# Conv then low-rank mixer on one core: eight-tile conv with shifted copies on GpSimd, eight output buffers, batch 0 in two pieces

## The chip, the core and the metric

The kernel runs on one core of a Trainium2 chip. Its engines are TensorE (PE, with weight loads shown as PEld), VectorE (DVE), ScalarE (ACT), GpSimd (POOL) and SyncE (SP). The metric is the time of one execution on the device in microseconds, as the median of several runs. A profile is one further execution, taken by the hardware profiler; its rows give durations of single instructions and what ended an engine's idle time.

## The reference

`x` is 8 batches of 4224 positions of 192 channels. First comes a causal convolution along the positions: 8 heads of 24 channels, 7 taps for each head, softmaxed. Then a mixer: a rank-32 product along the positions, added to its input, and a two-layer net along the channels, added again.

```python
w = exp(weight - max) / (sum + 1e-9)              # 8 heads x 7 taps
y[b, s, h, :] = sum_k w[h, k] * x_pad[b, s + k, h, :]   # 6 zeros ahead
h = y.transpose(0, 2, 1) @ U @ V                  # U: 4224 x 32, V: 32 x 4224
u = y + h.transpose(0, 2, 1)
out = u + maximum(u @ w_ch1, 0) @ w_ch2           # 192 -> 768 -> 192
```

## The kernel before, in words

**Tiles.** A batch is 33 tiles of 128 positions; 264 tiles in all, in 33 groups of 8. Everything after the load is bf16, sums are fp32 in PSUM. PSUM is one ring of eight banks (`bank`, line 55), handed out in program order, so that an instruction that wants a bank waits for the one that emptied it eight banks before.

**Load.** `x_part` (line 75) loads part of a batch from fp32 to bf16 on GpSimd's DMA queue. In SBUF, partitions 0 to 63 hold the blocks of 64 positions of the first half of the batch (32 blocks and one for the halo), partitions 64 to 127 those of the second (34 and one). A batch is four parts (`XP`, line 83); batch 0 is loaded and convolved in three pieces instead (`KP`, line 85, and `x_piece`). Three x buffers rotate. The parts of batches 2 to 7 are issued from the main loop, held until a certain matmul of W1 is done (`LOADS`, line 607).

**Conv** (line 297) is matmuls with a band matrix as the weights: for each head, one product for the block itself and one for the halo, the block before it (`halo`), for each half `r` and for even and odd blocks `c`. These are 64-by-64 tiles of the array, four (`r`, `c`) side by side; each has up to 17 blocks of 24 channels, 408 columns. That makes 8 matmuls a head and 64 a batch. Each head fills two banks, and `evac` copies them to `y_sb`, one on ACT and one on DVE (engines "AD").

**U product and h.** `tt_mm` (line 334) multiplies y by U in 33 small matmuls on 128-by-32 tiles; `tt_split` and `tt_sum` bring it to the form that h needs. `h_group` (line 448 on) makes the 8 tiles of h for one group (L425), and DVE adds y (L447) to give u. A DMA transpose on SP's queue turns u round for W1 (`transp`).

**W1 and W2.** `w1` (line 511) makes 36 matmuls of 512 columns for a group, with ReLU on ACT and DVE by a pattern (L530, L532). `w2` (line 537) makes two tiles at a time in 12 matmuls of 192 columns; DVE adds u into an output buffer (L551), and SP stores it (L558). Four output buffers rotate (line 51).

**Order.** It is written out by hand. Each entry of `SLOTS` (line 571) lists the groups for W1, the groups for W2, the convs that come between the two, and what is done ahead of which W2 step: `h` makes an h group, `t` the U product, `s` its sum. Slots 5 to 13 have three groups each (24 tiles); the convs of slots 5 to 10 are in `CONV`. Each engine works through its instructions in program order.

**Start.** 60 matmuls on zeros (`idle`, line 170) run first; the band is built; then three and two idle matmuls of 512 columns stand ahead of the first and second piece of batch 0 (lines 620 and 623).

Of the kernel before, what the change touches and what calls it, by code (L numbers as in the profile page):

```python
# [14 lines left out]
def kernel(  # L15
# [10 lines left out]
    nc = tc.nc  # L26
# [16 lines left out]
    ctx.enter_context(tc.manual_schedule())  # L43

    cst = ctx.enter_context(tc.tile_pool(name="cst", bufs=1))
    xs = ctx.enter_context(tc.tile_pool(name="xs", bufs=3))
    ys = ctx.enter_context(tc.tile_pool(name="ys", bufs=3))
    us = ctx.enter_context(tc.tile_pool(name="us", bufs=7))
    uts = ctx.enter_context(tc.tile_pool(name="uts", bufs=5))
    rls = ctx.enter_context(tc.tile_pool(name="rls", bufs=3))  # L50
    outs = ctx.enter_context(tc.tile_pool(name="outs", bufs=4))
    sml = ctx.enter_context(tc.tile_pool(name="sml", bufs=2))
    psp = ctx.enter_context(tc.tile_pool(name="psp", bufs=8, space=bass.MemoryType.PSUM))

# [14 lines left out]
    def x_tile(b):  # L69
        xt[b] = xs.tile([P, NB1 + 1, D], BF16, name="x_sb")  # L70
# [11 lines left out]

    XP = [(0, 1, 17), (0, 17, NB0 + 1), (1, 0, 18), (1, 18, NB1 + 1)]

    KP = [(0, 7), (7, 13), (13, NB1 // 2)]

    def x_piece(k):
        for r in range(2):
            k0, k1 = KP[k]
            k1 = min(k1, (NB0, NB1)[r] // 2)  # L90
            x_part(0, r, (1 - r if k == 0 else 2 * k0 + 1), 2 * k1 + 1)
# [25 lines left out]

    fp = cst.tile([P, P], I32, name="fp")
    nc.gpsimd.iota(fp[:], pattern=[[1, P]], base=P, channel_multiplier=-1)
    x_piece(1)  # L120

    efp = cst.tile([P, 4, P], I32, name="efp")
    nc.gpsimd.iota(efp[:], pattern=[[-1, 4], [1, P]], base=4 * P, channel_multiplier=-4)
# [8 lines left out]
    )  # L132
    nlast = NT * 32 - nfull * P
    nc.gpsimd.dma_start(out=Ur[0:nlast, nfull, :], in_=U4[nfull * P :, :])
    x_piece(2)


    V0_sb = cst.tile([32, 2 * GT * P], BF16, name="V0_sb")
# [155 lines left out]
            )  # L294


    def conv(b, h0, nh, rs, engs, k0=0, k1=NT):

        if yt[b] is None:
            yt[b] = ys.tile([P, NT, D], BF16, name="y_sb")  # L300
        nk = {r: min(k1, (NB0, NB1)[r] // 2) - k0 for r in rs}
        pp = {r: bank() for r in rs}
        w = nh * GS
        for hh in range(nh):
            h = h0 + hh
            for halo in range(2):
                for r in rs:
                    for c in range(2):
                        st = 1 - halo + c + 2 * k0
                        nc.tensor.matmul(  # L310
                            out=pp[r][HB * c : HB * c + HB, 0 : nk[r] * w].rearrange(
                                "p (k a) -> p k a", a=w
                            )[:, :, hh * GS : hh * GS + GS],
                            lhsT=band[HB * r : HB * r + HB, h, HB * halo : HB * halo + HB],
                            rhs=xt[b][
                                HB * r : HB * r + HB,
                                st : st + 2 * nk[r] - 1 : 2,
                                h * GS : h * GS + GS,
                            ],
                            start=(halo == 0),  # L320
                            stop=(halo == 1),
                            tile_position=(HB * r, HB * c),
                        )
        for n, r in enumerate(rs):
            j0 = NB0 // 2 * r + k0
            evac(
                engs[n % len(engs)],
                yt[b][:, j0 : j0 + nk[r], h0 * GS : h0 * GS + w],
                pp[r][:, 0 : nk[r] * w].rearrange("p (k a) -> p k a", a=w),
            )  # L330
# [55 lines left out]
            )  # L386

    def tt_done(b, p):
        t = sml.tile([P, D], BF16, name="tt_sb")
        nc.vector.tensor_copy(out=t[:], in_=p[:, 0:D])  # L390
        ttb[b] = t

# [167 lines left out]
    def held(ins, after):  # L560
        tc.add_manual_dep(
            ins.ins,
            after.ins.name,
            mybir.DependencyInfo(mybir.DependencyClass.Sync, mybir.DependencyReason.DATA),
            reason="load held back",
        )
# [2 lines left out]


    SLOTS = [
        ([0], [], [], {}),
        ([1], [0], [], {0: ["h0"], 1: ["h3"]}),
        ([2], [1], [(1, 0, 8)], {0: ["h1"], 1: ["t1"], 3: ["s1"], 4: ["h4"]}),
        ([3], [2], [(2, 0, 4)], {1: ["h5"]}),
        (
            [4, 5],
            [3, 4, 5],
            [(2, 4, 8)],
            {1: ["t2", "h6"], 3: ["s2"], 4: ["h7"], 7: ["h8"], 10: ["h9"]},  # L580
        ),
    ]
    CONV = {
        5: [(3, 0, 8)],
        6: [(4, 0, 8)],
        7: [(5, 0, 4)],
        8: [(5, 4, 8), (6, 0, 3)],
        9: [(6, 3, 8), (7, 0, 2)],
        10: [(7, 2, 8)],
    }  # L590
    SUMS = {5: (3, 5), 6: (4, 10), 8: (5, 2), 9: (6, 6), 10: (7, 10)}
    nh = 10
    for k in range(5, 14):
        gs = list(range(3 * k - 9, 3 * k - 6))
        at = {}
        for p in (1, 5, 9) if k == 5 else (2, 6, 10):
            if nh < NG:
                at.setdefault(p, []).append(f"h{nh}")
                nh += 1
        if k in SUMS:  # L600
            b, p = SUMS[k]
            at.setdefault(p, []).insert(0, f"t{b}")
            at.setdefault(p + 2, []).insert(0, f"s{b}")
        SLOTS.append((gs, gs, CONV.get(k, []), at))
    assert nh == NG

    LOADS = {2: [(1, 5), (1, 5), (2, 2), (2, 5)]}
    for b, g in ((3, 4), (4, 6), (5, 9), (6, 12), (7, 15)):
        LOADS[b] = [(g, 1), (g, 4), (g + 1, 1), (g + 1, 4)]

    def held(ins, after):
        tc.add_manual_dep(
            ins.ins,
            after.ins.name,
            mybir.DependencyInfo(mybir.DependencyClass.Sync, mybir.DependencyReason.DATA),
            reason="load held back",
        )


    idle(3, 512)  # L620
    for h in range(0, H, 2):
        conv(0, h, 2, [0, 1], "AD", *KP[0])
    idle(2, 512)
    for h in range(0, H, 2):
        conv(0, h, 2, [0, 1], "AD", *KP[1])
    u_layout()
    yT = yT_part(0)
    jb = NB0 // 2
    rest = [(KP[2][0], jb), (jb + KP[2][0], NT)]
    ps0 = bank()  # L630
    U4_sb, tf = tt_first(
        ps0, list(range(KP[2][0])) + list(range(jb, jb + KP[2][0])), rest
    )
    for h in range(0, H, 4):
        conv(0, h, 4, [0, 1], "AD", *KP[2])
    nc.tensor.matmul(out=ps0[:, 0:D], lhsT=R4f[:], rhs=tf[:], start=True, stop=False)
    tt_more(ps0, U4_sb, rest)
    tt_done(0, ps0)
    hT_part(0, yT, "AD")
    x_tile(1)  # L640
    x_zero(1, nc.gpsimd)
    for xp in XP:
        x_part(1, *xp)

    def do(what):
        n = int(what[1:])
        if what[0] == "h":
            h_group(n)
            if n > 1:
                transp(n)  # L650
        elif what[0] == "t":
            tt_split(n, tt_mm(n, range(NT)))
        else:
            tt_sum(n)

    for gs1, gs2, convs, at in SLOTS:
        for g in gs1:
            ends = w1(g, RELU0 if g < 2 else RELU)
            for b, blocks in LOADS.items():
# [6 lines left out]
            if g == 0:  # L666
                hT_part(1, yT_part(1), "AD")
                do("h2")
        n = sum(h1 - h0 for _, h0, h1 in convs)
        for b, h0, h1 in convs:  # L670
            for h in range(h0, h1):
                conv(b, h, 1, [0, 1], "AD" if n > 2 else "A")
        npc = 4 * len(gs2)
        for p in range(npc + 1):
            for what in at.get(p, []):
# [38 lines left out]
```

## Time and profile before

| what | value |
|---|---|
| time, median of 8 runs | 340.6 us (339.13 to 341.43) |
| the profiled execution's own time | 340.75 us |
| its span, first to last instruction | 339.0 us |
| granted TensorE clock, mean | 0.995 |
| POOL busy | 39.4 us (12%) |
| ACT busy | 160.5 us (47%) |
| start of the first W1 | 21.5 us |
| HBM read, written | 29.49 MB, 25.95 MB |

The page gives each engine's busy time as a share of the span. The chain of waits is followed back from the last instruction, at each step to what released it; its lines are start, length and the work. A row of a group gives the line, engine and operation, the tiles (output, then input), how many there were, then busy time in us and mean ns of one, then the engine's idle time just before them and what ended it. A matmul's own duration includes its way through the array, so that matmuls overlap; what one costs in a stream is read from the spacing of many. A row of DMA issues gives the count, the KB written by each, and the median time from issue to landing.

The DMA engines are busy for almost all of the time until about 190 us, and about half afterwards, when no x is left to load.

### The profile page before, as it was taken

The page shows a single profiled execution, that of the slowest core. Times are in us where ns is not written, and L with a number is a line of the kernel's source. Part 1 is how long each engine was busy: PE and PEld are TensorE (multiplying, and loading weights), DVE is VectorE, ACT ScalarE, POOL GpSimd, SP SyncE. Part 2 cuts the span into 40 slices and gives each one's busy share as a digit, 9 for nine tenths or more (in the row PEclk, how much of TensorE's full clock was granted, in tenths as well). Part 3 has the DMA queues.
Part 4 walks back from the last instruction along what each step waited for, and adds up shares of the span by engine and source line. Part 5 has one row for each costly group of instructions (what it writes and reads, how often), then busy time and mean ns, then how long its engine had stood idle before and what let it go on. Part 6 is the DMA issues. An engine that isn't in the chain of part 4 may idle for free.

```text
span 339.0 us, 9771 instructions
## 1 busy us (share of the span) xinstructions
PE 326.0 (96%) x4111; PEld 234.4 (69%) x4111; DVE 279.8 (83%) x571; ACT 160.5 (47%) x327; POOL 39.4 (12%) x65
## 2 busy tenths in 40 slices
PE   6789999999999999999999999999999998999995
PEld 6545675678557856965964884697887587487595
DVE  5736999988888888988898889888898887886863
ACT  1648446550492097059039308705912911922910
POOL 8660210120120040012012000000000000000000
PEclk9979999999999999999999999999999999999999
DMA  8999994699895999789799596069049238429135
GB/s 106 192 165 140 167 214 125 93 216 260 188 211 99 233 190 130 203 191 204 135 261 188 101 236 140 2 185 235 2 114 240 70 86 241 96 71 256 48 117 165
DMA packets 122940, 53.54 MB, mean 158 GB/s; under 512 B 87792, under 2 KB 122864, under 8 KB 122896
## 3 DMA queue, kind: packets, MB, share of 16 engines
q1 hardware_dynamic: 84672, 38.18, 45.2%
q0 software_dynamic: 38224, 14.73, 37.3%
q8 instruction: 32, 0.52, 0.6%
q14 instruction: 12, 0.10, 0.1%
HBM read 29.49 MB, written 25.95 MB: 164 GB/s over the span
## 4 chain that ended last, share of the span: by engine, by line
PE 82%; DVE 7%; DMA 6%; ACT 2%; issue 1%; POOL 1%; DVEq 0%; POOLq 0%
PE ps L519 37%; PE ps L543 33%; PE ps L310 7%; DMA out_dram<-out_sb 6%; DVE out_sb L551 2%; PE ps L425 2%; PE ps L340 2%; DVE u_sb L447 1%; ACT rl_sb L530 1%; DVE y_sb L274 1%; DVE pr L223 1%; DVE rl_sb L532 1%; POOL x_sb L78 1%; PE ps L477 0%; PE ps L173 0%
## 5 line engine op out<-in xcount | busy, mean ns | idle before, releaser
L530 ACT ACTIVATE rl_sb<-ps 128x512 bf16<-128x512 f32 x235 | 126.0, 603 | 109.5 <-PE ps L519 88.1
L543 PE MATMUL ps<-W_sb,rl_sb 128*128 128x192 bf16 x1584 | 139.1, 246 | 1.8 <-DVE out_sb L551 1.8
L543 PEld LDWEIGHTS <-rl_sb 128*128 128x128 bf16 x1584 | 128.9, 98 | 10.7 <-issue 10.5
L519 PE MATMUL ps<-uT,W_sb 64*128 64x512 bf16 x1188 | 135.0, 379 | 1.3 <-DVE uT L274 0.7
L532 DVE TENSOR_SCALAR rl_sb<-ps 128x512 bf16<-128x512 f32 x161 | 103.5, 686 | 16.9 <-PE ps L519 16.5
L519 PEld LDWEIGHTS <-W_sb 64*128 64x128 bf16 x1188 | 66.7, 94 | 65.2 <-issue 8.5
L551 DVE TENSOR_TENSOR out_sb<-ps,u_sb 128x384 f32<-128x384 f32 (+1 forms) x133 | 70.0, 550 | 26.0 <-DMA out_dram<-out_sb 12.2
L447 DVE TENSOR_TENSOR u_sb<-y_sb,ps 128x192 bf16<-128x192 bf16 (+1 forms) x168 | 66.2, 459 | 0.0
L78 POOL DMA_DIRECT2D x_sb<-in_x_dram x34 | 28.2, 835 | 139.9 <-PE ps L519 125.8
L274 DVE CAST y_sb<-ps 128x408 bf16<-128x408 f32 (+3 forms) x66 | 32.5, 559 | 2.8 <-PE ps L310 2.8
L310 PE MATMUL ps<-x_sb,band 64*64 64x384 bf16 (+5 forms) x640 | 26.5, 298 | 0.0
L272 ACT ACTIVATE y_sb<-ps 128x384 bf16<-128x384 f32 (+2 forms) x66 | 26.0, 507 | 0.5 <-PE ps L310 0.3
L310 PEld LDWEIGHTS <-band 64*64 64x64 bf16 x640 | 18.3, 106 | 9.0 <-issue 7.0
L354 ACT ACTIVATE tt_hi<-ps 128x192 bf16<-128x192 f32 x7 | 2.3, 331 | 41.1 <-PE ps L340 41.1
L425 PE MATMUL ps<-tt_sb,V_sb 32*128 32x192 bf16 x264 | 12.2, 246 | 0.2 <-DVE y_sb L274 0.2
L425 PEld LDWEIGHTS <-V_sb 32*128 32x128 bf16 x264 | 4.6, 92 | 6.3 <-issue 5.5
L173 PE MATMUL ps<-zz 128*128 128x128 bf16 (+1 forms) x65 | 6.4, 274 | 1.2 <-DVE zz L168 1.2
L340 PE MATMUL ps<-y_sb,U_sb 128*32 128x192 bf16 x257 | 7.2, 247 | 0.0
L173 PEld LDWEIGHTS <-zz 128*128 128x128 bf16 x65 | 5.2, 122 | 1.4 <-DVE zz L168 1.2
L340 PEld LDWEIGHTS <-U_sb 128*32 128x32 bf16 x257 | 5.3, 96 | 1.2 <-issue 1.1
L355 DVE TENSOR_TENSOR tt_lo<-ps,tt_hi 128x192 bf16<-128x192 f32 x7 | 2.5, 355 | 3.7 <-ACT tt_hi L354 3.7
L240 ACT ACTIVATE band<-ps 32x152 bf16<-32x152 f32 x8 | 2.3, 288 | 3.2 <-PE ps L231 3.1
(57 smaller groups left out, 46.1 us busy)
## 6 DMA issues: line engine op xcount, KB each, us to landing
out_dram<-out_sb SPq DMA_DIRECT2D x131, 192.0 KB, 2.8
x_sb<-in_x_dram POOLq DMA_DIRECT2D x14, 384.0 KB, 7.4
x_sb<-in_x_dram POOLq DMA_DIRECT2D x7, 432.0 KB, 8.7
x_sb<-in_x_dram POOLq DMA_DIRECT2D x7, 408.0 KB, 9.0
x_sb<-in_x_dram POOLq DMA_DIRECT2D x2, 288.0 KB, 6.0
uT<-u_sb SPq DMA_TRANSPOSE x31, 4.0
W_sb<-in_moe_w_ch_dram POOLq DMA_DIRECT2D x2, 192.0 KB, 6.1
x_sb<-in_x_dram POOLq DMA_DIRECT2D x1, 360.0 KB, 6.1
```

The lines of the kernel that those rows point to most:

```text
L78: return nc.gpsimd.dma_start(out=xt[b][HB * r : HB * r + HB, s0:s1, :], in_=x[b, blk * HB : (blk + s1 - s0) * HB, :].rearrange("(j p) d -> ...
L272: nc.scalar.activation(out=out, in_=in_, func=ACT.Copy)
L274: nc.vector.tensor_copy(out=out, in_=in_)
L310: nc.tensor.matmul(out=pp[r][HB * c : HB * c + HB, 0 : nk[r] * w].rearrange("p (k a) -> p k a", a=w)[:, :, hh * GS : hh * GS + GS], lhsT=b ...
L340: nc.tensor.matmul(out=p[32 * c : 32 * c + 32, o : o + D], lhsT=U_sb[:, j // 4, j % 4, :], rhs=yt[b][:, j, :], start=(n < 4), stop=(n + 4 ...
L425: nc.tensor.matmul(out=banks[pr][:, a * D : (a + 1) * D], lhsT=V_sb[32 * q : 32 * q + 32, (j // 8) * 2 + j % 2, :], rhs=ttb[b][32 * q : 32 ...
L447: nc.vector.tensor_tensor(out=u_group(g)[:, i : i + n, :, hf, :], in0=yt[b][:, run[0] : run[0] + n, :].rearrange("p n (c k) -> p n c k", c=3),
L519: last = nc.tensor.matmul(out=pp[hf][:], lhsT=W1_sb[HB * hf : HB * hf + HB, c, m * P : (m + 1) * P], rhs=uTt[g][HB * hf : HB * hf + HB, :, ...
L530: nc.scalar.activation(out=rl[:, m, hf, :], in_=pp[hf][:], func=ACT.Relu)
L532: nc.vector.tensor_scalar_max(out=rl[:, m, hf, :], in0=pp[hf][:], scalar1=0.0)
L543: nc.tensor.matmul(out=cps[:, a * D : (a + 1) * D], lhsT=rlt[g][:, m, hf, (i + a) * P : (i + a + 1) * P], rhs=W2_sb[:, m, :], start=(m == ...
L551: nc.vector.tensor_tensor(out=o[:, 0:n, :].rearrange("p n (c k) -> p n c k", c=3), in0=cps[:, 0 : n * D].rearrange("p (n c k) -> p n c k", ...
```

## The change

- Eight output buffers instead of four; three for `tt_sb` instead of two.
- Batch 0 in two pieces instead of three: `KP` is now (0, 13) and (13, 17). The second piece is loaded where the third was. Instead of the five idle matmuls of 512 columns, 30 of 128 columns stand between the band and the first piece.
- Two x buffers instead of three, and one buffer `xb_sb` for a second copy of a batch.
- Batch 1 keeps the old conv. Batches 2 to 7 take `conv32`: a block of 64 positions is cut into four quarters of 32 outputs. A quarter needs 32 + 6 positions, which lie in one 64-row block of x, or in the second copy, so that one product with a 64-by-32 tile is enough: the halo product is gone. Eight tiles (four quarters, two halves) lie side by side; 8 matmuls a head and 64 a batch as before, with half as many columns of the array each.
- The second copy is made on GpSimd by `x_shift`: partitions 0 to 31 of each half hold the block, partitions 32 to 63 the one before it. `x_shift` also issues the loads of the batch after, two parts behind its first copies and two behind its last. `band2` is the matching rearrangement of the band.
- The convs no longer stand between W1 and W2 but within W2, in pieces of two or three heads, with ACT and DVE sharing the eviction by the patterns AAD and AD. The places of `h`, `t` and `s` move.

```diff
-    xs = ctx.enter_context(tc.tile_pool(name="xs", bufs=3))
+    xs = ctx.enter_context(tc.tile_pool(name="xs", bufs=2))
+    xbs = ctx.enter_context(tc.tile_pool(name="xbs", bufs=1))
...
-    outs = ctx.enter_context(tc.tile_pool(name="outs", bufs=4))
+    outs = ctx.enter_context(tc.tile_pool(name="outs", bufs=8))
...
-    KP = [(0, 7), (7, 13), (13, NB1 // 2)]
+    KP = [(0, 13), (13, NB1 // 2)]
...
+    def x_shift(b):
+        xbt[b] = xbs.tile([P, NB1, D], BF16, name="xb_sb")
+        nc.gpsimd.tensor_copy(out=xbt[b][:, 0:NB0, :], in_=xt[b][:, 1 : NB0 + 1, :])
+        nc.gpsimd.tensor_copy(
+            out=xbt[b][HB : HB + QB, NB0:NB1, :],
+            in_=xt[b][HB : HB + QB, NB0 + 1 : NB1 + 1, :],
+        )
+        more = XP if b + 1 < B and xt[b + 1] is None else []
+        if more:
+            x_tile(b + 1)
+            x_zero(b + 1, nc.gpsimd)
+        for xp in more[:2]:
+            x_part(b + 1, *xp)
+        for r in range(2):
+            q = slice(HB * r + QB, HB * r + HB)
+            nc.gpsimd.tensor_copy(
+                out=xbt[b][q, 0 : (NB0, NB1)[r], :], in_=xt[b][q, 0 : (NB0, NB1)[r], :]
+            )
+        for xp in more[2:]:
+            x_part(b + 1, *xp)
+
+    def conv32(b, h0, nh, engs):
...
+        for n in range(nh):
+            h = h0 + n
+            hs = slice(h * GS, h * GS + GS)
+            pp = [bank(), bank()]
+            for cg in range(4):
+                t, w, st = (
+                    (xt[b], band[:, h, QB : 2 * QB], 1 + cg // 2)
+                    if cg % 2
+                    else (xbt[b], band2[:, h, :], cg // 2)
+                )
+                for r in range(2):
+                    hr = slice(HB * r, HB * r + HB)
+                    nc.tensor.matmul(
+                        out=pp[r][QB * cg : QB * cg + QB, 0 : nk[r] * GS],
+                        lhsT=w[hr],
+                        rhs=t[hr, st : st + 2 * nk[r] - 1 : 2, hs],
+                        start=True,
+                        stop=True,
+                        tile_position=(HB * r, QB * cg),
+                    )
...
     SLOTS = [
...
-        ([2], [1], [(1, 0, 8)], {0: ["h1"], 1: ["t1"], 3: ["s1"], 4: ["h4"]}),
-        ([3], [2], [(2, 0, 4)], {1: ["h5"]}),
+        ([2], [1], {0: ["d1", "h1"], 1: ["t1"], 3: ["s1"], 4: ["h4", "x2"]}),
+        ([3], [2], {1: ["h5"]}),
         (
             [4, 5],
             [3, 4, 5],
-            [(2, 4, 8)],
-            {1: ["t2", "h6"], 3: ["s2"], 4: ["h7"], 7: ["h8"], 10: ["h9"]},
+            {
+                0: ["h6"],
+                1: ["c2:0:3:AAD"],
+                2: ["c2:3:3:AD"],
+                3: ["c2:6:2:AD", "x3"],
+                4: ["h7", "t2"],
+                6: ["s2"],
+                7: ["h8"],
+                10: ["h9"],
+            },
         ),
...
+        if k == 5:
+            at = {0: [hs[0]], 3: ["c3:0:3:A"], 4: ["c3:3:2:AAD"], 5: [hs[1]],
+                  7: ["c3:5:3:AD", "x4"], 9: ["t3"], 10: ["s3"], 11: [hs[2]]}
+        elif k < 10:
+            b = k - 2
+            at = {
+                0: [hs[0]],
+                4: [f"c{b}:0:3:AAD"],
+                5: [f"c{b}:3:3:AAD"],
+                6: [hs[1]],
+                8: [f"c{b}:6:2:AD"] + ([f"x{b + 1}"] if b + 1 < B else []),
+                10: [hs[2], f"t{b}"],
+                12: [f"s{b}"],
+            }
+        else:
+            at = {0: [hs[0]], 4: [hs[1]], 8: [hs[2]]}
...
     LOADS = {2: [(1, 5), (1, 5), (2, 2), (2, 5)]}
-    for b, g in ((3, 4), (4, 6), (5, 9), (6, 12), (7, 15)):
-        LOADS[b] = [(g, 1), (g, 4), (g + 1, 1), (g + 1, 4)]
...
-    idle(3, 512)
-    for h in range(0, H, 2):
-        conv(0, h, 2, [0, 1], "AD", *KP[0])
-    idle(2, 512)
-    for h in range(0, H, 2):
-        conv(0, h, 2, [0, 1], "AD", *KP[1])
+    idle(30, P)
+    for h in range(H):
+        conv(0, h, 1, [0, 1], "AD", *KP[0])
...
+    band2 = cst.tile([P, H, QB], BF16, name="band2")
...
+    for r in range(4):
+        q = slice(QB * r, QB * r + QB)
+        nc.gpsimd.tensor_copy(
+            out=band2[q], in_=band[q, :, HB * (r % 2) : HB * (r % 2) + QB]
+        )
```

In the last parts, `d1` is the old conv of batch 1, `c3:0:3:A` is `conv32` of batch 3 from head 0, three heads, eviction pattern A, and `x4` is `x_shift(4)`.

## The prediction

> **What bounds the kernel now.** I read the first and fourth parts of the page, then the chain of waits, then the groups by form, the waits, the timeline around the two longest holes of PE, and last the rows of POOL and of the DMA issues.
>
> ```profile
> PE 326.0 (96%) x4111; PEld 234.4 (69%) x4111; DVE 279.8 (83%) x571; ACT 160.5 (47%) x327; POOL 39.4 (12%) x65
> PE 82%; DVE 7%; DMA 6%; ACT 2%; issue 1%; POOL 1%; DVEq 0%; POOLq 0%
> ```
>
> PE carries the chain. DVE, at 83%, is the next candidate; POOL is nearly free. One conv slot of the main loop, from the chain of waits (start, length, what):
>
> ```profile
> 117.82 12.02 PE ps L519 x108
> 129.84 3.27 PE ps L310 x61
> 133.11 2.09 PE ps L543 x24
> 135.19 0.28 PE ps L425 x8
> 135.47 4.07 PE ps L543 x48
> ...
> 143.88 0.85 PE ps L340 x33
> ```
>
> PE runs without a hole: W1 (L519), Conv (L310), W2 (L543), h (L425), the U product (L340). Conv's 64 matmuls (a few records are missing) take 3.27 us, 51 ns each, while the rows by form give one alone about 330 ns; so the four 64-by-64 tiles do run beside each other, a round of four in 204 ns. In W2, 48 matmuls take 4.07 and 24 take 2.09: 82.5 ns each, plus 0.11 us for coming back from another tile shape. The slots as W1 starts delimit them (87.19, 117.82, 147.19, 173.99, 203.18, 231.98, 260.28, 286.31, 310.82) sum to 173.1 us for slots 5 to 10, which hold the convs of batches 3 to 7. Slot 11, with no conv, is 26.0.
>
> The holes that remain, from the waits and the timeline:
>
> ```profile
> DVE out_sb L551 <- DMA out_dram<-out_sb: 12.2, 12, 1.9
> ```
>
> ```profile
> 82.49 2.14 PE L543 MATMUL ps<-W_sb,rl_sb 128*128 128x192 bf16 x24 [0.56 <-DVE out_sb L551]
> ...
> 284.24 2.14 PE L543 MATMUL ps<-W_sb,rl_sb 128*128 128x192 bf16 x24 [0.96 <-DVE out_sb L551]
> ```
>
> DVE waits 12.2 us for output buffers, but PE feels only 0.56 and 0.96 of it, and about 0.5 in slot 13, where W1 takes 12.28 instead of 11.8.
>
> **The change, part by part.**
>
> *Conv on eight tiles.* Each head still takes 8 matmuls, each with 384 or 408 columns, but on eight tiles that run at once instead of four tiles twice. A round of eight should last as a round of four does now, 204 ns: 64 matmuls then cost 8 x 0.204 = 1.6 us. No row shows 64-by-32 tiles. Upper end: no more than four run at once, 3.27 us as now. Lower end: the columns alone, about 1.4. The row nearest is L340, 128-by-32 tiles, four at once: 33 matmuls in 0.85, 26 ns each, so narrow tiles do overlap; I take 1.6. The conv now comes in three pieces within W2, each with an entry and a 0.11 return, where before it had one: about 0.4 more. So 2.0 instead of 3.27.
>
> *A conv slot.* The slot above lasts 29.37 us; 29.37 - 3.27 + 2.0 = 28.1. Five of them (slots 5 to 9) and slot 10 without conv (slot 11 less its 0.96 hole, 25.1) make 165.6, against 173.1.
>
> *DVE in such a slot.* 15 ReLUs x 0.686, 12 output sums x 0.552, three h groups of about 1.95, six conv evictions x 0.571 (eight before; two go to ACT, which waits through W2), tt 0.7: 26.9 us of 28.1. Just hidden. In W2 it has 16.6 us of work in 16.3, and ends in W1, where it has 1.5 to spare.
>
> *GpSimd's copies.* Per batch: 6144 + 384 + 6144 + 6528 = 19,200 elements per partition in four instructions, all before that batch's first eight-tile matmul. The trace has no copy on POOL; the nearest are
>
> ```profile
> L123 POOL IOTA efp<- 128x512 int32 x1 | 0.6, 592 | 0.0
> ...
> L119 POOL IOTA fp<- 128x128 int32 x1 | 0.2, 250 | 0.0
> ```
>
> Their slope is (592 - 250)/384 = 0.89 ns an element, and 0.14 us fixed; but an iota doesn't read. [...] I take the row, 0.89: 17.1 + 0.6 = 17.7 us. Between these copies stand two x loads of the next batch (0.84 each, row L78) and a memset, 0.2: about 19.5 us from the start of a shift to its end. The last two loads come behind it.
>
> ```profile
> x_sb<-in_x_dram POOLq DMA_DIRECT2D x7, 432.0 KB, 8.7
> x_sb<-in_x_dram POOLq DMA_DIRECT2D x7, 408.0 KB, 9.0
> ```
>
> The next shift reads all of its batch, so it can't start before the last of these has landed: 0.85 + 9.0 = 9.9 us later. That is a loop of 29.4 us against a slot of 28.1, but it begins with slack. Batch 2's last part is issued at 43.3 and lands at 52.3; its shift ends at 71.8, those of batches 3 to 7 at 101.2, 130.6, 160.0, 189.4 and 216.9 (the last has no loads in it). PE reaches those convs (slot start + W1 11.9 + one h 0.3 + the W2 pieces ahead, 3.3 or 4.2; for batch 2 slot 4's start, 62.3 less a half conv, with two W1 groups, 7.9, and one W2 piece) at 70.4, 102.7, 131.7, 159.8, 187.9, 216.0. What is late: 1.4 at batch 2, at most 1.5 at batch 6. PE is in order, so all W2 behind the conv would wait; 1.5 us goes on the sum. Slots 5 to 10: 167.1, a gain of 6.0.
>
> Could DVE lock POOL out? [...] I take nothing, and leave the rest to the slow rival.
>
> *Slots 2 to 4.* Batch 1 keeps the old conv. Slot 3 loses half of batch 2's conv, -1.5. Slot 4 (62.3 to 87.2, 24.9 us) now has all of it and is DVE's: 10 ReLUs 6.9, 12 sums 6.6, four h groups 8.0, seven conv evictions 4.0, tt 0.7, in all 26.2, +1.3. The 1.4 for the copies lies beside that. Sum -0.2.
>
> *Output buffers.* With eight, a store has twice as long. I count what PE felt outside the slots already summed: 0.96 and 0.5, -1.4; next there is W2 itself. The end stays: the last sum starts at 335.16, with its store behind it.
>
> *Batch 0.* The first piece now needs 53 blocks of x instead of 29. These are the same bytes in the same order: the timeline shows POOL waiting for an x load until 11.71, so pieces 0 and 1 of today are there at about 11.7. Today PE has done the first piece by then and ends the second at 13.3. After: 30 idle matmuls from 9.5 (1.6 to 2.5 us, by the 512-column ones and by row L173), conv at 11.8 with 312 columns, about 2.5, to 14.3; its eviction, 8 x 0.47 on DVE, ends at 15.8, where today U's layout has ended at 14.9. But PE today stands still until 16.0 with nothing that the profile shows, so +0.3. Ends: -1.8 if the low clock at 20 to 31 us (0.84) doesn't come back, +2 if the standstill moves with the work.
>
> *At no price:* band2 (four 256-element copies, 1.5 us, in POOL's 11.6 us idle before 33.9), the third tt buffer, the smaller x pool. Batches 3 to 7 lose their own load places; that is in the loop above.
>
> Sum: -6.0 - 0.2 - 1.4 + 0.3 = -7.3. The profiled run took 340.75 (span 339.0), near the median 340.6: 333.4.
>
> **The rivals.**
>
> *The copies are late (slower).* The loop adds up over six batches. With copies of c ns, batch 7's shift ends at 99.9 + 6 x (19.2 c + 2.46). The gain of 8.8 before lateness is used up when that reaches 224.8: at c = 0.96 ns, or, at 0.89, when the loads take 11.4 us instead of 9.9. At 1.0 ns the time is about 346, at 1.5 ns 403. For it: 0.96 is close to the row, and the last two loads go out back to back among stores (the DMA share in slots 5 to 8 is about 1.0). [...] Chance 0.25, of which 0.10 for the far end.
>
> *DVE becomes the bound:* evictions and sums in one stage, 16.6 us in 16.3; if each conv slot loses 1 us, 338. Against: ACT takes ten of sixteen. Chance 0.10.
>
> *Eight tiles don't overlap:* conv stays at 3.27 with its three pieces, 5 x 1.67 given back less the 1.5 of lateness: 340. L340 speaks against it. Chance 0.04.
>
> *More than forecast:* copies at 0.86 or less (-1.5), the low clock gone (-1.8): 330. Chance 0.20. The forecast itself: 0.41.
>
> **Numbers.** Faster: 0.41 + 0.20 + 0.10 = 0.71; slower 0.25; same 0.04 (within 0.3%, about what a measurement of this kernel can tell). The range goes from 326 (better still, by the lower conv end) to 350, leaving out the far copies and the edges.
>
> **What would show it.** Right: 64-by-32 matmuls at about 25 ns each; POOL copies of 6144 elements at about 5.5 us; conv slots at 28 to 28.5; L551 no longer waiting for stores; PE holes of at most 1.5 us before a conv. Wrong: PE standing before the conv for the copy, in each slot more; or DVE without a gap through W2 and W1.

## The result, and the profile after

The changed kernel takes 335.4 us, median of 11 runs (332.92 to 337.12), against 340.41 us for the kernel before, median of 32 runs (338.58 to 341.98). The ratio is 0.9845, with an interval of 0.982 to 0.9871: 5.0 us faster by the medians. The profiled execution took 333.61 us (span 331.7 us, granted clock 0.995), 7.1 us less than the one before.

The page of the changed kernel: busy times, the chain by engine, GpSimd's two groups of copies, and the landing times of stores and transposes (the last number, us).

```profile
PE 319.4 (96%) x4072; PEld 218.1 (66%) x4072; DVE 274.8 (83%) x558; ACT 166.4 (50%) x340; POOL 139.5 (42%) x91
PE 87%; DMA 5%; DVE 3%; ACT 2%; issue 0%; POOL 0%; SPq 0%; DVEq 0%; POOLq 0%
...
L316 POOL COPY xb_sb<-x_sb 32x6144 bf16<-32x6144 bf16 (+1 forms) x12 | 65.5, 5462 | 0.6
L303 POOL COPY xb_sb<-x_sb 128x6144 bf16<-128x6144 bf16 x6 | 31.8, 5304 | 50.2 <-PE ps L340 27.8
...
out_dram<-out_sb SPq DMA_DIRECT2D x131, 192.0 KB, 3.2
...
uT<-u_sb SPq DMA_TRANSPOSE x31, 5.4
```

PE still carries the chain. POOL now has 139.5 us of work, yet is on the chain for less than half a per cent: its copies come in time. Stores and transposes take longer than before (2.8 us and 4.0 us in the same rows before).

The chain of waits of the changed kernel, once around the hole in slot 4 and once for a conv slot (slot 6):

```profile
60.24 7.07 DMA uT<-u_sb
67.31 0.05 issue
67.36 4.06 PE ps L578 x36
...
116.98 11.76 PE ps L578 x108
...
129.21 4.07 PE ps L602 x48
133.28 0.64 PE ps L340 x19
133.92 1.10 PE ps L602 x12
135.02 0.71 PE ps L340 x17
135.72 1.10 PE ps L602 x12
...
139.24 0.47 PE ps L340 x11
```

In slot 6 (W1 is L578, W2 L602, conv L340) PE has no hole, and the three conv pieces sum to 1.82 us, where the conv before took 3.27. In slot 4, W1 of group 5 waits for a transpose that took 7.07 us; PE's hole there is 2.51 us, the longest new one. It is the only wait of W1 for a transpose in this profile (us in total, times, longest):

```profile
PE ps L578 <- DMA uT<-u_sb: 2.5, 1, 2.5
```

The starts of W1 in both profiles cut the span into stages:

| stage | predicted | before, us | after, us | measured |
|---|---|---|---|---|
| up to W1 of slot 2 | +0.3 | 38.35 | 38.42 | +0.1 |
| slots 2 to 4 | -0.2 | 48.84 | 50.31 | +1.5 |
| slots 5 to 10 | -6.0 | 173.02 | 165.63 | -7.4 |
| slots 11 to 13 and the end | -1.4 | 78.79 | 77.34 | -1.5 |
| span | -7.3 | 339.0 | 331.7 | -7.3 |

The sum fits to a tenth, but two of its terms miss by 1.4 to 1.7 us in opposite directions; and the median moved by 5.0, not 7.3. The experiments ask what each part is worth, and where the rest went.

### The profile page after: what moved, and what is told of

The parts are those of the page before. It is cut to its first block, busy times and chain, and to the rows that moved or that the text cites. A ratio compares the mean times of both kernels' runs of the same rounds, so it can differ in the third digit from the quotient of the medians.

```text
span 331.7 us, 9715 instructions
## 1 busy us (share of the span) xinstructions
PE 319.4 (96%) x4072; PEld 218.1 (66%) x4072; DVE 274.8 (83%) x558; ACT 166.4 (50%) x340; POOL 139.5 (42%) x91
## 4 chain that ended last, share of the span: by engine, by line
PE 87%; DMA 5%; DVE 3%; ACT 2%; issue 0%; POOL 0%; SPq 0%; DVEq 0%; POOLq 0%
PE ps L602 40%; PE ps L578 37%; PE ps L340 3%; DMA x_sb<-in_x_dram 3%; PE ps L484 3%; DMA uT<-u_sb 2%; PE ps L399 2%; DVE y_sb L274 2%; ACT y_sb L272 1%; ACT rl_sb L589 1%; DVE u_sb L506 1%; DVE rl_sb L591 1%; PE ps L536 0%; PE ps L369 0%; PE ps L455 0%
## 5 line engine op out<-in xcount | busy, mean ns | idle before, releaser
L602 PE MATMUL ps<-W_sb,rl_sb 128*128 128x192 bf16 x1584 | 140.3, 246 | 0.1
L578 PE MATMUL ps<-uT,W_sb 64*128 64x512 bf16 x1188 | 133.2, 380 | 3.2 <-DMA uT<-u_sb 2.5
L602 PEld LDWEIGHTS <-rl_sb 128*128 128x128 bf16 x1584 | 128.3, 98 | 11.3 <-issue 10.7
L578 PEld LDWEIGHTS <-W_sb 64*128 64x128 bf16 x1188 | 58.3, 95 | 73.9 <-issue 5.6
L610 DVE TENSOR_TENSOR out_sb<-ps,u_sb 128x384 f32<-128x384 f32 (+1 forms) x133 | 69.9, 548 | 17.5 <-PE ps L602 16.8
L316 POOL COPY xb_sb<-x_sb 32x6144 bf16<-32x6144 bf16 (+1 forms) x12 | 65.5, 5462 | 0.6
L303 POOL COPY xb_sb<-x_sb 128x6144 bf16<-128x6144 bf16 x6 | 31.8, 5304 | 50.2 <-PE ps L340 27.8
L272 ACT ACTIVATE y_sb<-ps 128x384 bf16<-128x384 f32 (+3 forms) x79 | 32.3, 502 | 36.6 <-PE ps L340 34.6
L274 DVE CAST y_sb<-ps 128x408 bf16<-128x408 f32 (+2 forms) x53 | 26.6, 552 | 2.7 <-PE ps L369 2.7
L484 PE MATMUL ps<-tt_sb,V_sb 32*128 32x192 bf16 x264 | 13.1, 247 | 0.3 <-DVE y_sb L274 0.2
L340 PE MATMUL ps<-xb_sb,band 64*32 64x384 bf16 x192 | 12.4, 332 | 0.1
L340 PE MATMUL ps<-x_sb,band 64*32 64x384 bf16 x192 | 12.1, 332 | 0.0
L484 PEld LDWEIGHTS <-V_sb 32*128 32x128 bf16 x264 | 4.9, 92 | 9.5 <-issue 9.5
L173 PE MATMUL ps<-zz 128*128 128x128 bf16 x90 | 7.0, 252 | 1.2 <-DVE zz L168 1.2
L369 PE MATMUL ps<-x_sb,band 64*64 64x312 bf16 (+3 forms) x192 | 7.2, 277 | 0.6 <-DMA x_sb<-in_x_dram 0.6
L340 PEld LDWEIGHTS <-band 64*32 64x32 bf16 x384 | 4.4, 89 | 4.5 <-issue 3.0
```

What stands on the lines that cost most here:

```text
L272: nc.scalar.activation(out=out, in_=in_, func=ACT.Copy)
L274: nc.vector.tensor_copy(out=out, in_=in_)
L303: nc.gpsimd.tensor_copy(out=xbt[b][:, 0:NB0, :], in_=xt[b][:, 1 : NB0 + 1, :])
L316: nc.gpsimd.tensor_copy(out=xbt[b][q, 0 : (NB0, NB1)[r], :], in_=xt[b][q, 0 : (NB0, NB1)[r], :])
L340: nc.tensor.matmul(out=pp[r][QB * cg : QB * cg + QB, 0 : nk[r] * GS], lhsT=w[hr], rhs=t[hr, st : st + 2 * nk[r] - 1 : 2, hs], start=True, ...
L484: nc.tensor.matmul(out=banks[pr][:, a * D : (a + 1) * D], lhsT=V_sb[32 * q : 32 * q + 32, (j // 8) * 2 + j % 2, :], rhs=ttb[b][32 * q : 32 ...
```

## The experiments

In the experiments with spread loads or further lines, line numbers are a few higher than in the changed kernel (W1 L578 becomes L579 or L580, W2 L602 becomes L603 or L604, and the output sum L610 L611 or L612). Ratios are to the kernel before, run on the same chip.

### The changed kernel again

> The changed kernel once more, unaltered, as the control of this chip. The theory (eight tiles give 6 to 8 us in slots 5 to 10, and slots 2 to 4 lose 1.6 to a DMA transpose): median 5 us below the kernel before, profile with slots 5 to 9 at 28.2 us each. What is open: the first profile stood 7.1 us below the kernel before, the medians only 5.0. If that is the number of low-clock stretches of TensorE (one, 3.4 us at half clock, in both profiles), a slow profile shows two such stretches and the same slots; if it is the transpose at slot 4, the hole ahead of the fifth W1 group changes from run to run.

No edit. Measured: 336.68 us (333.89 to 337.56, 6 runs), before 340.89, ratio 0.9872 [0.9835, 0.991]. The profile (335.9 us) again has a hole of 2.5 us ahead of W1 of group 5, and another loss in slot 8, which lasts 29.57 us instead of 28.02. Its chain there:

```profile
190.19 0.56 DVE out_sb L610
190.75 0.27 DVE y_sb L274
191.01 9.37 DMA out_dram<-out_sb
```

One store took 9.37 us, and with eight buffers DVE still waited for it. So the first profile was one of the better executions: the hole of slot 4 comes back, and others of this kind come and go. That is one reason why the median moved less than the profile.

### Four output buffers

> The changed kernel with four output buffers instead of eight. Theory: the buffers are worth what TensorE felt of them, 1.4 us outside the conv slots and up to 0.5 inside: 1.5 to 2.5 us slower than the changed kernel, VectorE's wait for stores back at about 12 us. Rival, that most of the gain came from the buffers: 4 to 5 us slower, back at the kernel before.

```diff
-    outs = ctx.enter_context(tc.tile_pool(name="outs", bufs=8))
+    outs = ctx.enter_context(tc.tile_pool(name="outs", bufs=4))
```

Measured: 367.24 us (366.03 to 369.03), ratio 1.0786 [1.0749, 1.0823]. Waits (us in total, times, longest):

```profile
DVE out_sb L610 <- DMA out_dram<-out_sb: 34.7, 12, 8.0
...
PE ps L484 <- DVE out_sb L610: 13.3, 3, 5.8
...
PE ps L578 <- DVE out_sb L610: 7.9, 2, 7.0
```

DVE waits 34.7 us for stores, up to 8.0 at a time, and PE then waits for DVE in W1 (L578) and in h (L484). The longest of these waits ends with the landing of one store, as the chain shows:

```profile
86.64 10.24 DMA out_dram<-out_sb
...
97.00 0.57 DVE out_sb L610
```

Inside the change the buffers are worth 31 us, not 1.4, and neither expectation came near: the rest of the change makes stores late enough to need them. Not all of the 31 us is waiting. In four stretches behind PE's waits, 20.5 us in all, the granted clock was 0.50, so up to 10 us is PE at half speed (an estimate, half of the 20.5).

### The old tiles at the new places

> The changed kernel with the old conv (64-by-64 tiles, block and halo product) at the same places, in the same pieces and with the same eviction engines; GpSimd still makes its copies, but nothing reads them. Theory, that the gain is TensorE's time in conv: 1.67 us for each of six batches, 8.5 to 10 us slower than the changed kernel, so 3 to 5 us slower than the kernel before. Rival, that the gain came from spreading conv over W2 and from giving evictions to ScalarE: no more than 3 us slower than the changed kernel.

```diff
-            conv32(int(b), int(h0), int(n), engs)
+            for i in range(int(n)):
+                two = engs[2 * i % len(engs)] + engs[(2 * i + 1) % len(engs)]
+                conv(int(b), int(h0) + i, 1, [0, 1], two)
```

The copies of `x_shift` are still made, though nothing reads them. Measured: 343.44 us (341.88 to 344.33, 8 runs), ratio 1.007 [1.0037, 1.0104]: 6.8 above the changed kernel on the same chip, between the two expectations. Without the eight tiles the change is a loss of 2.6 us, buffers and all.

### The first two loads of one batch later

> The changed kernel with one thing moved: in the shift of batch 2 the first two loads of batch 3 are issued between the two quarter copies instead of ahead of them, 5.5 us later. Theory: the transpose of group 5 took 7.07 us instead of some 4 because these loads ran beside it; with them later TensorE's 2.5 us hole ahead of the fifth W1 group goes, and the time falls by 1.5 to 2.5 us. Rival, that the transpose is slow because of the stores or of its own queue: no change within 0.5 us. What it may cost: batch 3's shift ends later, but it had 6 us in hand.

```diff
+        if b != 2:
             for xp in more[:2]:
                 x_part(b + 1, *xp)
...
+            if b == 2 and r == 0:
+                for xp in more[:2]:
+                    x_part(b + 1, *xp)
```

The hole of 2.5 us ahead of W1 of group 5 went. But batch 3's loads landed later (up to 14.6 us after their issue), its shift came late, and conv waited for the copy, as the timeline shows:

```profile
103.30 0.50 PE L344 MATMUL ps<-xb_sb,band 64*32 64x408 bf16 x1 [2.95 <-POOL xb_sb L317]
```

The hole had moved, and behind it the granted clock was 0.50 from 103 to 107 us. The six runs lie between 331.51 and 340.79 us, too far apart for a ratio, so the median (338.58 us) decides nothing. What stays is that these loads make this hole.

### The kernel before, with eight output buffers

> The kernel before with eight output buffers and nothing else. The prediction put this part at 1.4 us. In the changed kernel four buffers instead of eight cost 31 us, so the buffers can be worth much or little depending on the order around them. Theory, that stores are late only where x loads run in pairs beside transposes, as the changed order makes them: 1 to 2 us faster than the kernel before. Rival, that stores are late in the old order too and four buffers hide a large loss: over 5 us faster.

The edit is that of the buffers alone, 4 to 8, in the kernel before. Measured: 335.1 us (334.44 to 337.37), before 340.6, ratio 0.9853 [0.9819, 0.9888]. One number gives as much as the whole change, as the rival expected. By stages its profile (span 332.7) stands to before at -1.5 up to slot 2, -1.0 in slots 2 to 4, -2.2 in slots 5 to 10, -1.6 behind. The first is not the buffers': a stretch of low clock is missing in this profile, which has 1.00 from 21.4 to 25.0 us where the one before has 0.53 (see the experiment with more idle matmuls). About 4.9 remain, 2.2 of it in slots that the prediction counted under the conv.

### The loads of a shift spread out

> The changed kernel with the four loads of a shift spread over it: one ahead of the first copy, one ahead of each of the two quarter copies, one behind the last, instead of two pairs. The copies and their order stay. Theory: a pair of loads slows the transposes and the stores behind them on SP's queue, and this makes the 2.5 us hole ahead of the fifth W1 group and most of the spread between runs; spread out, the longest transpose falls below 8 us (10.8 and 11.2 in the two profiles) and the median by 1.5 to 3 us. Rival, that transposes are slow through the sum of the load bytes, however they are spread: median within 1 us of the changed kernel.

```diff
+        def load():
+            if more:
+                x_part(b + 1, *more.pop(0))
-        xbt[b] = xbs.tile([P, NB1, D], BF16, name="xb_sb")
+        load()
         nc.gpsimd.tensor_copy(out=xbt[b][:, 0:NB0, :], in_=xt[b][:, 1 : NB0 + 1, :])
...
-        for xp in more[:2]:
-            x_part(b + 1, *xp)
+        load()
         for r in range(2):
...
-        for xp in more[2:]:
-            x_part(b + 1, *xp)
+            load()
```

The four loads go out singly: ahead of the first copy, ahead of each quarter copy, behind the last. Measured: 331.53 us (329.6 to 331.93), before 340.6, ratio 0.9724 [0.9693, 0.9755]. The intervals don't overlap with those of the changed kernel: issued as they were, in pairs, the loads cost 4 to 5 us of the median. The run changes the times of the loads along with the pairing, and does not tell the two apart. The chain at W1 of group 5:

```profile
60.06 5.10 DMA uT<-u_sb
...
65.20 4.06 PE ps L580 x36
```

The transpose takes 5.10 us instead of 7.07, and the hole is 0.54 instead of 2.51. The longest transpose still took 9.9 us, where less than 8 was expected. Slots 5 to 9 are those of the changed kernel to 0.02 us (28.18 against 28.19 in slot 6); what went is the hole of slot 4, 2.0 us between the two profiles. That the other 2 to 3 us of the median are collisions like that of slot 8 fits the repeated profile, but no trace shows it run by run.

### All evictions of conv one on ACT, one on DVE

> The changed kernel with all eight-tile evictions alternating between ScalarE and VectorE: 8 of 16 of a batch on VectorE instead of 6. Theory, TensorE bound: VectorE then has 28.0 us of work in a slot of 28.2, and the time rises by no more than 1.5 us. Rival, VectorE bound (the second rival of the prediction): each slot with a conv grows by the 1.1 us of two more evictions, 5.5 to 7 us in all.

```diff
-                4: [f"c{b}:0:3:AAD"],
-                5: [f"c{b}:3:3:AAD"],
+                4: [f"c{b}:0:3:AD"],
+                5: [f"c{b}:3:3:AD"],
```

The same in slots 4 and 5. Measured: 336.16 us (333.94 to 337.28, and one run of 339.93 that the ratio leaves out), ratio 0.9859 [0.9822, 0.9896], the same as the changed kernel. DVE gets two evictions more in a slot, 2 x 0.571 us, and slots 6, 8 and 9 of its profile last 28.1 to 28.2 us as before. DVE is not the bound. Slots 5 and 7 last 29.3 and 29.6 us. There the chain shows two more collisions of the kind of the repeated profile, a transpose and a store:

```profile
85.46 11.97 DMA uT<-u_sb
...
164.68 7.96 DMA out_dram<-out_sb
```

### One more copy in each shift

> The changed kernel with one more GpSimd copy of 6144 elements in each shift, ahead of the loads (it writes what the first copy wrote, once more): a shift lasts 24.0 us instead of 18.6. The loop of the prediction, with the 9.6 us from the end of a shift to the landing of its last load: batch 7's shift ends some 24 us after TensorE reaches its conv, so the time is 20 to 25 us above the changed kernel. Rival, that copies have room to spare because the loads and copies overlap more than the loop says: under 5 us.

```diff
+        nc.gpsimd.tensor_copy(out=xbt[b][:, 0:32, :], in_=xt[b][:, 1 : 33, :])
```

It repeats the first copy, 5.3 us. Measured: 355.55 us (354.79 to 359.54, 4 runs), ratio 1.0474 [1.0414, 1.0534]. The wait that the prediction's slow rival spoke of, from the waits of this kernel:

```profile
PE ps L341 <- POOL xb_sb L317: 17.3, 6, 5.4
```

PE waits for the copies six times, in five of the six batches (twice in batch 2, not in batch 3), 17.3 us in all, and is at half clock for 20.5 us behind these waits. So 5.3 us more in a shift cost about 20, and the copies are as close to the edge as the prediction had it. But the loop is not of copies and loads alone. There is one `xb_sb`, so a shift also waits until the conv of the batch before has read it. The chain shows such a start for batch 7, whose last load had come in 2 us before:

```profile
216.90 0.56 PE ps L341 x11
...
217.51 5.31 POOL xb_sb L303
```

### Spread loads, four output buffers

> The kernel with spread loads, with four output buffers instead of eight. Of the 31 us that four buffers cost in the changed kernel, the theory puts most on pairs of x loads: they slow a transpose to 7 us and more, SP's queue holds the stores behind it, VectorE stands for lack of a buffer, and TensorE behind it. With the loads spread the longest wait for a buffer falls from 8.0 us to under 4, and the cost from 31 us to 8 to 18. Rival, that the new order (conv within W2) needs more than four buffers whatever the loads do: 25 us or more above the kernel with spread loads and eight buffers.

The spread loads, with `bufs=4`. Measured: 351.86 us (350.13 to 353.36), before 340.85, ratio 1.033 [1.0296, 1.0363].

```profile
DVE out_sb L612 <- DMA out_dram<-out_sb: 25.6, 17, 3.5
```

So some 10 of the 31 us go with the pairs, and 20 remain, more than the theory's 8 to 18. By the starts of W1 most of the loss against spread loads with eight buffers is in slot 5 (37.1 us against 28.2), slot 7 (31.4 against 28.2) and slot 8 (31.3 against 28.0): slots with loads. The last run below takes this up.

### Spread loads, and more idle matmuls

> The kernel with spread loads, and 22 more matmuls of 128 columns on zeros in the two waits just ahead of the first W1 group (8 while VectorE rounds tt, 14 while the first u is brought to bf16), their result unused. Theory: the low clock that nearly every profile shows from 21.4 to 25 us (0.55) follows from how little TensorE does from 17 to 21 us, and costs 1.7 us where it comes (0.993 against 0.999 in the runs with spread loads: 331.6 against 329.8). With the waits filled the clock stays above 0.997 in most runs and the median falls by 1 to 1.7 us. Rival, that the low clock doesn't hang on these waits: same clock, same time or up to 0.3 us longer.

```diff
+    def warm(n):
+        for _ in range(n):
+            nc.tensor.matmul(
+                out=spare[0][:, 0:P], lhsT=zz[:, 0:P], rhs=zz[:, 0:P], start=True, stop=True
+            )
...
     tt_done(0, ps0)
+    warm(8)
     hT_part(0, yT, "AD")
+    warm(14)
```

`spare` is the pair of banks of batch 0's last conv. Measured: 330.32 us (329.5 to 334.15), ratio 0.9711 [0.967, 0.9752]: the fastest version, though only 1.2 below spread loads alone, within their intervals. What the fill does can be seen at the first W1, in the changed kernel, in this one, and in spread loads with old tiles (the next run, without the fill):

```profile
21.40 5.86 PE L578 MATMUL ps<-uT,W_sb 64*128 64x512 bf16 x36 [0.51 <-DVE uT L274]
```

```profile
21.76 4.06 PE L581 MATMUL ps<-uT,W_sb 64*128 64x512 bf16 x36
```

```profile
21.36 4.29 PE L580 MATMUL ps<-uT,W_sb 64*128 64x512 bf16 x36 [0.51 <-DVE uT L274]
```

In the changed kernel the granted clock is 0.50 for 3.41 us of this W1, and the same 36 matmuls take 1.6 to 1.8 us more. All six runs with the fill had a mean clock of 0.997 to 1.0; those of the changed kernel had 0.987 to 1.0, those of spread loads 0.993 to 0.999. But five of the six runs with old tiles had 0.997 to 1.0 too, with the same hole ahead of W1: a kernel without the fill can keep the clock. The last section says when it was lost.

### Spread loads, old tiles

> The kernel with spread loads, with the old conv on 64-by-64 tiles at the same places (GpSimd still copies, nothing reads it). Theory: with the collisions gone the tiles alone are worth the 1.67 us a batch of the prediction, 9 to 10 us for six batches: 340.5 to 341.5. With the pairs of loads still there the same exchange cost 6.8. Rival, that part of the saving on TensorE is hidden by VectorE and evictions anyway: 6 to 7.5 us here too, about 338.

Spread loads, with the edit of the old tiles. Measured: 338.01 us (336.99 to 339.1), ratio 0.9917 [0.989, 0.9944], 6.5 above spread loads with eight tiles. Slot by slot the profiles differ by 1.26 to 1.32 us in each of the six slots with eight tiles, 7.7 in all; 1.4 us goes back because this profile kept the clock at the first W1 and that of spread loads did not. Its chain in slot 6 (conv is L371, W2 L604):

```profile
132.28 1.16 PE ps L371 x24
133.44 1.10 PE ps L604 x12
134.54 1.16 PE ps L371 x24
...
139.16 0.81 PE ps L371 x16
```

The same three pieces as in the changed kernel's chain take 1.16 + 1.16 + 0.81 = 3.13 us here and 0.64 + 0.71 + 0.47 = 1.82 there. Eight tiles save 1.31 us a batch in the place where they stand, not the theory's 1.67, and the slots show all of it: nothing is hidden by DVE, as the rival had it.

### Four output buffers and no loads of batches 3 to 7

> Four output buffers with spread loads (351.9 us) lose some 19 us in the profile against eight (slot 5: 37.1 us instead of 28.2; slots 7 and 8: 31.4 and 31.3 instead of 28.2 and 28.0), all in slots whose W2 has x loads beside it. This kernel has four buffers and no loads of batches 3 to 7 at all: they convolve batch 2's x again, so this part of the computation is left out. All copies on GpSimd remain. Theory (loads beside the stores make four buffers too few): slots 5 to 9 at 28.2 to 28.7, DVE's waits for stores under 6 us in all, time 329 to 334. Rival (the order of conv and W2 leaves DVE no slack, so that four buffers stall whatever is loaded): slot 5 stays over 31, DVE's waits for stores over 15 us, time 343 or more.

```diff
-        more = list(XP) if b + 1 < B and xt[b + 1] is None else []
-        if more:
-            x_tile(b + 1)
-            x_zero(b + 1, nc.gpsimd)
+        more = []
+        if b + 1 < B:
+            xt[b + 1] = xt[b]
```

Measured: 335.4 us (334.78 to 336.29, 4 runs), before 341.21, ratio 0.9838 [0.9796, 0.9881]. Batches 3 to 7 convolve batch 2's x again, so the loads and that part of the computation are left out. Four buffers are enough for slots 6 to 9 when nothing is loaded; the starts of W1 in its timeline show slots 6 to 8 at 28.3, 28.2 and 28.1 us:

```profile
115.95 11.83 PE L579 MATMUL ps<-uT,W_sb 64*128 64x512 bf16 x108
144.21 11.83 PE L579 MATMUL ps<-uT,W_sb 64*128 64x512 bf16 x108
172.40 11.83 PE L579 MATMUL ps<-uT,W_sb 64*128 64x512 bf16 x108
200.49 11.83 PE L579 MATMUL ps<-uT,W_sb 64*128 64x512 bf16 x108
```

DVE's waits for stores (us in total, times, longest):

```profile
DVE out_sb L611 <- DMA out_dram<-out_sb: 12.8, 9, 3.7
```

They are 12.8 us, more than the 6 that the theory allowed. Of these, 10.0 fall after 248 us, where no kernel here loads any x, and 2.75 in the conv slots, both in slot 5, which lasts 29.6 us. So the theory holds for slots 6 to 9. It missed slot 5 (28.2 to 28.7 expected), DVE's waits and the time (329 to 334 expected): slot 5 and the last slots stall with four buffers even without these loads. The landing times of the transposes, min, median and max, in the changed kernel and in this one, say the same:

```profile
DMA to landing us min/median/max: 3.7/5.4/10.8
```

```profile
DMA to landing us min/median/max: 3.7/3.9/6.5
```

## Why the prediction was right, and where it was not

**The eight tiles.** Right. Forecast: 3.27 to 2.0 us a batch, a gain of 1.27; measured 1.31 with pieces against pieces, and 6.5 us in the whole kernel for the exchange alone. Conv slots were to last 28.1 and last 28.0 to 28.3. Eight tiles do overlap. One matmul lasts 322 to 344 ns, but the next head's eight begin 0.16 to 0.17 us after the last, as the first rows of three heads in slot 4 show:

```profile
75.27 0.34 PE L340 MATMUL ps<-xb_sb,band 64*32 64x384 bf16 x2
...
75.44 0.32 PE L340 MATMUL ps<-xb_sb,band 64*32 64x384 bf16 x1
...
75.60 0.32 PE L340 MATMUL ps<-xb_sb,band 64*32 64x384 bf16 x1
```

That is about 21 ns a matmul. The gain of 1.31 us is eight such rounds of 0.164, eight instead of sixteen. So the sum was right and its parts were not: a round was put at 0.204, which was the whole conv before, 3.27, over its sixteen rounds. Eight rounds take 1.3 us, and the other 0.5 of the 1.82 goes into starting three pieces; the returns in W2 come on top.

**The copies.** The rate was nearly right: 5.30 us for 6144 elements, 0.863 ns each, where the sum used 0.89 ns and 0.14 us. The 0.86 and 1.5 ns an element that the prediction's rivals name had no row behind them; the three large copies of a shift (6144, 6144 and 6528 elements) took 0.862 to 0.863. Nor had the "nothing" that it took for DVE locking POOL out, but it held: the six whole-width copies took 5.304 us each, the shortest like the longest, with DVE busy for 29.6 of these 31.8 us, so DVE held none of them up.

A shift took 18.7 us instead of 19.5, and the next one could begin 9.5 us behind it instead of 9.9 (starts at 168.03 and 196.24 us, the end between them at 186.7). The loop so lasted 28.2 us instead of 29.4, no longer than a slot, and the lateness that was to grow from batch to batch did not: in slots 5 to 9 PE reaches the conv 2.7 to 6.0 us after the shift has ended. The step that failed is "1.5 us goes on the sum".

The loop also had a leg that the prediction left out, the wait for `xb_sb`. Of the six shifts of the changed kernel three began, by the profile, when the conv before them ended (27.8 us of waiting; in two of the three the last packet of the loads had come only 0.5 us earlier), two when a load had landed (15.1), and one is put down to a matmul of h. The mechanism of the slow rival is real, as the run with one more copy shows. Its price starts when the delays of all shifts together use up the lead of 2.7 us; with a loop as long as a slot nothing renews that lead (an estimate from 28.2 against 28.2).

**Slots 2 to 4.** "Sum -0.2" was wrong: +1.5 in the profile, with the hole of 2.5 ahead of W1 of group 5 in it. Slot 3 gave the forecast -1.5; slot 4 without its hole lasts 25.4 us, not DVE's 26.2. The prediction counted what the two pairs of loads cost GpSimd's queue (0.84 each) and when they land, and left out what they do to others: they now go out in W1 and W2, beside SP's transposes and stores, and the transpose of group 5 takes 7.07 us, where the median before was 4.0. The sum gave it no cost at all. The two runs with the loads moved and the run with none show that it is the loads: holes went, moved or came with them (ahead of W1 of group 5 2.51 us in the changed kernel and 0.54 with the loads spread; with two loads later 2.95 ahead of a conv; with none PE waits for no transpose).

**The output buffers.** The step "I count what PE felt outside the slots already summed: 0.96 and 0.5, -1.4" held as arithmetic (-1.5 there), but it is no measure of what the buffers do. Alone they give 5.5 us. Part of the gain went to the account of the conv: the slots' sum before, 173.1, is 1.1 us more than five times the slot shown (29.37) and 25.1, and with eight buffers alone these slots take 2.2 less. And the demand is not fixed: with the loads beside the stores, going back to four costs 31 us. The prediction never asked what four buffers would have cost in the changed kernel.

**From 7.3 to 5.0.** The profile met the sum by luck: a loss that the sum missed (1.7) and a loss that did not come (1.4) nearly cancelled. The median is some 2 us worse than that profile. The repeated profile shows one way: a store of 9.37 us, and slot 8 lasts 1.5 us longer. Stretches at half clock are another: the runs of the changed kernel above 336 us had mean clocks of 0.987 to 0.993, those below 334.1 had 0.995 to 1.0. A hole can bring such a stretch (in the run with the loads later 0.50 from 103 to 107 us, behind a hole of 2.95), so the two go together, and how they share those 2 us was not measured.

**The balance.** Buffers alone -5.5, tiles alone -6.5, together -12. The change gives -5.0, with spread loads -9.1. The 2.9 still missing is what the rest of the change costs: spread loads with old tiles are slower by that much than the kernel before with eight buffers. By the profiles of these two, which are 3.6 us apart, 1.2 us is in slots 5 to 9, where the conv is cut into pieces within W2, 1.8 in slots 2 to 4 and 0.7 behind slot 10; these are single profiles, and it was not tried part by part.

**The rivals.** DVE as the bound: refuted by the evictions moved to it. Eight tiles that don't overlap: refuted by the chain. Copies late: not here, but about 3 us away. "More than forecast", 330 us, asked for faster copies and for the low clock to go; in the changed kernel the clock stayed as it was, and 330.32 us came only with spread loads and the fill.

**Batch 0.** +0.3 forecast, the first W1 at 21.4 us against 21.5. Right within what can be told.

## What to carry to other kernels

When a change moves loads, cost them for the transfers that run beside them at the new time: here pairs of loads of some 400 KB, issued beside transposes and stores, cost nearly as much as the whole change gained, and issuing the same loads singly, at other times, gave it back. Test a cheap part alone, in the old kernel and in the new: the buffers were worth 1.4 us in the sum, 5.5 alone and 31 inside the change. A loop over a buffer has a leg for each of its users: here not only the loads but also the conv that reads `xb_sb`. A forecast that meets the profile by terms that cancel has not been confirmed; cut the span into stages and compare each.

## What the runs showed of the hardware

- A copy on GpSimd of 32 partitions took as long as one of 128, 5.3 us for 6144 elements each. Splitting this copy by partitions would save nothing (an estimate from these two rows); 32 x 384 elements took 0.50 us. With the two shapes of L316 apart:

```profile
L303 POOL COPY xb_sb<-x_sb 128x6144 bf16<-128x6144 bf16 x6 | 31.8, 5304 | 50.2 <-PE ps L340 27.8 <-DMA x_sb<-in_x_dram 15.1 <-PE ps L484 7.2
L316 POOL COPY xb_sb<-x_sb 32x6144 bf16<-32x6144 bf16 x6 | 31.8, 5297 | 0.3
```

- In the run with four buffers (the changed kernel with `bufs=4`) a transpose stood 6.68 us in SP's queue, and the two stores behind it went out only afterwards. DVE's longest wait for a buffer, 8.0 us, ends at the same moment, but not through these two: it ends with the store issued at 86.64 us, ahead of the transpose, which took 10.24 us to land.

```profile
86.64 3.51 SPq L617 DMA_DIRECT2D out_dram<-out_sb  x3
90.24 6.68 SPq L525 DMA_TRANSPOSE uT<-u_sb  x1
97.01 1.05 SPq L617 DMA_DIRECT2D out_dram<-out_sb  x2
```

- The granted clock fell to half for 3.41 us at the first W1; PE had stood for 1.0 us of the 3.41 us ahead (changed kernel; window and its length, busy time and matmuls of PE and PEld, busy time and instructions of DVE, ACT and POOL, granted clock, DMA share, GB/s):

```profile
18.36:21.77 3.41, 2.39 (x19) 1.19 (x20) 1.84 (x6) 1.26 (x4) 3.41 (x6) 1.00 1.06 120
21.77:25.18 3.41, 3.41 (x19) 1.46 (x19) 0.93 (x2) 1.68 (x3) 2.33 (x6) 0.50 1.59 191
```

The idle time alone does not decide. Spread loads with old tiles had the same 2.39 us of work in the 3.41 us ahead of 22.58 us and kept the clock. In all fourteen profiles the clock changes on a grid of 3.41 us that begins elsewhere in each (in the changed kernel at 4.70, 21.77 and 25.18 us: 17.07 is five times 3.41). Six profiles lost the clock here; in them a step of the grid lay between 0.1 us before and 1.0 us after the start of the first W1. Seven without the fill kept it; their nearest steps lay 0.24 us before and 1.2 us after. With the fill a step lay 0.24 us after, and the clock stayed (PE busy for 5.33 of the 5.40 us up to 21.4 us, against 4.38 in the changed kernel). So where the grid falls is what sets the runs that lost the clock apart from those that kept it, as far as these profiles go; why the clock falls at such a step was not measured.
